# The scores' factor of 1/8 moves from the keys into the exponential for 52 of 64 heads

## The chip, the core and the metric

The kernel runs on one core of a Trainium2 chip. The core has five engines that run their own instruction streams and wait for one another through semaphores: TensorE (PE in the profile, matrix products; PEld is its loading of stationary operands), VectorE (DVE), ScalarE (ACT), GpSimd (POOL), and SyncE (SP, which here only issues DMAs). SBUF is the working memory of 128 partitions, PSUM the eight banks that TensorE writes. The metric is device time of one execution in microseconds, lower is better; a run has several executions, and their median is compared.

## The reference

The program computes causal block attention and then a mixing layer with a feed-forward network, all in fp32:

```python
scores = (1 / sqrt(64)) * q @ k.T            # 8 batches x 8 heads, 576 x 576, head size 64
scores = where(block_i >= block_j, scores, -1e9)        # blocks of 64 positions
scores = scores - max(scores, -1)
attn = exp(scores);  attn = attn / (sum(attn, -1) + 1e-9)
x = attn @ v                                 # heads side by side: 576 x 512 per batch
u = x + (x^T U V)^T                          # rank 32
out = u + relu(u @ w_ch1) @ w_ch2            # 512 -> 2048 -> 512
```

## The kernel before

**Two-part numbers.** TensorE is kept at its fast fp32r rate: an fp32 operand is split into a rounded part and a remainder (names with 1/2, h/l or hi/lo), and a product is two or three fast products. The first twelve heads (h < FS = 12) don't split q and k; their scores are one slower fp32 product out of `raw`. The 52 heads from the thirteenth on do split them.

**A head's chain.** Head h of the 64 goes through these steps, each of which is one task or a few:

- `split_qk` (L881): a DMA brings q and k, transposed, side by side into `raw` (64 partitions x 1152). For the later heads ScalarE rounds q into `q2` (L906), multiplies the half of `raw` that holds k by SCALE = 0.125 in place (L909), and rounds that into `k1` (L911). GpSimd forms the remainders `q1` (L912) and `k2` (L913), 64x576 each. Two DMAs copy `q2` and `k1` to the lower 64 partitions. The lower half of `raw` holds ones and -2^30, so that the product of one array of 128 rows adds the mask.
- `softmax` (L937): four groups of query tiles in the order (4), (3), (2), (1, 0); tile i has 128 queries (tile 0 has 64) and 128 i + 64 keys. TensorE forms the scores in a PSUM bank (L966, L967); VectorE takes the negated maximum of each row into one column of `mx`, 128 partitions x 5 (L980); ScalarE takes exp(score + `mx` column) into `p` and sums the rows into `ss` (L991).
- `normalise` (L1001): VectorE adds the 1e-9 and inverts the sums (L1007, L1008); GpSimd multiplies `p` by them (L1017).
- `transpose` (L1029, products L1050): TensorE transposes `p`; ScalarE and VectorE bring it back to SBUF as `ph` (L1027) and `pl` (L1069).
- `apply_v` (L1079, L1109): the product with v; ScalarE and VectorE join its two halves (L1115, L1117). After each second head, `mix` (L1121) does the rank-32 layer for that pair (L1134 to L1168).

**What fills TensorE.** The feed-forward network of the sixteen chunks of 288 tokens runs in two halves of the hidden layer. The first half (`ffn_chunk`, L465 and L488, banks bf and bg) is cut into tasks of six products, and these stand beside the attention as work of the lowest priority for TensorE. What of it is left when the last head is done runs alone. Then follows the second half (`block_products`, L659), whose weights are fetched and prepared (L345, L547 to L551) after the last head.

**What sets the order.** The program is written out by a planner. Every step is entered with `add(engine, ns, priority, function, reads, writes)`; `Plan.issue` (L165) then goes through time with the estimated durations `ns` and picks for each engine, whenever it is free, the ready task of the smallest priority number. The instructions are emitted in that order, so each engine's queue is fixed at build time, and engines work their queues strictly in order. A task with `port=True` or on GpSimd is never started, in the planner's account, while another such one runs. So one changed task can deal the order anew for everything behind it, on every engine.

Of the kernel before, what the change touches and what calls it, by code (L numbers as in the profile page):

```python
# [12 lines left out]
AF = mybir.ActivationFunctionType  # L13
# [4 lines left out]
S = 576  # L18
# [9 lines left out]
SCALE = 0.125  # L28
# [18 lines left out]
FS = 12  # L47
# [90 lines left out]
class Plan:  # L138
# [8 lines left out]
    def add(self, engine, ns, prio, fn, reads=(), writes=(), hold=(), after=0, port=False):  # L147

        n = len(self.tasks)
        deps = set()  # L150
        for b in reads:
            deps.update(b.writers)
            b.readers.append(n)
        for b in hold:
            deps.update(b.readers, b.writers)
        for b in writes:
            deps.update(b.readers, b.writers)
            b.writers, b.readers = [n], []
        deps.discard(n)
        slots = {b for b in (*reads, *writes) if b.pool is not None}  # L160
        for b in slots:
            b.users += 1
        self.tasks.append((engine, ns, prio, fn, deps, after, slots, port or engine == "POOL"))
# [76 lines left out]
def _act(n, sbuf=False):  # L240
    return (93 if sbuf else 52) + 0.833 * n


def _dve(n):
    return 69 + 1.042 * n
# [9 lines left out]
def attention_then_mixer(  # L255
# [10 lines left out]
    nc = tc.nc  # L266
# [8 lines left out]
    add = plan.add  # L275
# [537 lines left out]
    mx_r = [b.split(5) for b in ring(ap, 2, [P, 5], F32, "mx")]  # L813
# [23 lines left out]
    for r in vr_r:  # L837
        nc.vector.memset(r[:, 10, :], 0.0)
    for j in range(2):
        nc.vector.memset(ss_r[j][:, :, 0], 1.0)  # L840
        nc.vector.memset(ss_r[j][:, :, 1], 1e-9)
    for i, r in enumerate(pt_r):
# [38 lines left out]
    def split_qk(h, pr):  # L881
        raw, q1, k1, q2, k2 = (r[h % 2] for r in (raw_r, q1_r, k1_r, q2_r, k2_r))

        def fetch():
            if h:
                nc.sync.dma_start(out=raw[0:64, :], in_=qk[h])
            else:
                for a in (S, 0):
                    nc.sync.dma_start(out=raw[0:64, a : a + S], in_=qk[h, :, a : a + S])

        if h in (FS - 2, FS - 1):

            for n, (x, o) in enumerate(((q2, 0), (k2, S))):
                add(
                    "DVE", _dve(S) / 2, pr, lambda x=x, o=o: nc.vector.tensor_copy(x[64:P, :], raw[64:P, o : o + S]),
                    [raw], [x],
                )
        add("SP", 820, pr, fetch, writes=[raw], after=DL)
        if h < FS:
            add(  # L900
                "ACT", _act(S, True), pr,
                lambda: nc.scalar.activation(raw[0:64, S : 2 * S], raw[0:64, S : 2 * S], AF.Copy, scale=SCALE), [raw], [raw],
            )
            return
        top = slice(0, 64)
        add("ACT", _act(S, True), pr, lambda: nc.scalar.copy(q2[top], raw[top, 0:S]), [raw], [q2])  # L906
        add(
            "ACT", _act(S, True), pr,
            lambda: nc.scalar.activation(raw[top, S : 2 * S], raw[top, S : 2 * S], AF.Copy, scale=SCALE), [raw], [raw],  # L909
        )  # L910
        add("ACT", _act(S, True), pr, lambda: nc.scalar.copy(k1[top], raw[top, S : 2 * S]), [raw], [k1])  # L911
        add("POOL", 1380, pr, lambda: nc.gpsimd.tensor_sub(q1[top], raw[top, 0:S], f32(q2[top])), [raw, q2], [q1])  # L912
        add("POOL", 1380, pr, lambda: nc.gpsimd.tensor_sub(k2[top], raw[top, S : 2 * S], f32(k1[top])), [raw, k1], [k2])  # L913

        add("SP", 600, pr, lambda: nc.sync.dma_start(out=f32(q1[64:P]), in_=f32(q2[top])), [q2], [q1], after=DL)
        add("SP", 600, pr, lambda: nc.sync.dma_start(out=f32(k1[64:P]), in_=f32(k1[top])), [k1], [k1], after=DL)
# [20 lines left out]
    def softmax(h, tiles, pr):  # L937

        q1, k1, q2, k2, ss, mx = (r[h % 2] for r in (q1_r, k1_r, q2_r, k2_r, ss_r, mx_r))
        raw = raw_r[h % 2]  # L940
# [36 lines left out]
        for i, at in parts:  # L977
            add(
                "DVE", _dve(P * i + 64), pr,
                lambda i=i, at=at: nc.vector.tensor_reduce(  # L980
                    out=mx[: P if i else 64, i : i + 1], in_=view(i, at), op=ALU.max, axis=AX.XY if wide else AX.X,
                    negate=True,
                ),
                [bank], [mx.parts[i]],
            )
        for i, at in parts:
            pt, rows = pt_r[i][h % PB[i]], P if i else 64

            def exponentials(i=i, at=at, pt=pt, rows=rows):
                out = pt[:rows, : P * i + 64]  # L990
                nc.scalar.activation(  # L991
                    out.rearrange("p (j k) -> p j k", j=2) if wide else out, view(i, at), AF.Exp,
                    bias=mx[:rows, i : i + 1], accum_out=ss[:rows, i, 0:1],
                )

            add(
                "ACT", _act(P * i + 64) + 188, pr, exponentials, [bank, *(mx.parts[i] for i in tiles)],
                [pt, ss.parts[i]],
            )
# [189 lines left out]
    for h in range(NH):  # L1189
        pr = 1000.0 * h  # L1190
# [79 lines left out]
```

## Time and profile before

| | before |
|---|---|
| median of 3 runs | 1183.15 us (1181.67 to 1183.31) |
| the profiled execution | 1182.37 us, of which its span is 1180.6 us |
| granted TensorE clock, whole span | 1.00 |
| start of the mixing layer's last product (L1163), the attention's end on TensorE | 657.2 us |
| start of the second half's first product (L659) | 819.9 us |

The profile's rows give, for a group of instructions of one line, engine and tile, the number (x), the busy time, the mean duration of one in ns, and the idle time of the engine just before them with what ended it. A line that is given "out<-in" names the tiles that are written and read; sizes are partitions x elements. The windows view gives for a stretch of the span each engine's busy time in us and its number of instructions in brackets. TensorE's busy time is to be read with care: products overlap in its pipeline and their ends are modelled, so it counts as busy in small waits too; the distance from one product's start to the next one's shows more.

### The profile page before, as it was taken

How to read it: one execution, taken by the hardware profiler on the slowest of the kernel's cores; microseconds unless marked ns; L12 is line 12 of the kernel's file. 1: busy time of each engine (PE TensorE's matmuls, PEld its weight loads, DVE VectorE, ACT ScalarE, POOL GpSimd, SP SyncE). 2: the span in 40 equal slices, each digit the busy share in tenths (PEclk: the TensorE clock that was granted, in tenths of full speed). 3: DMA queues.
4: the chain of work that ended last, by engine and by line, in shares of the span. 5: the costliest groups of instructions: out<-in, count | busy, mean ns of one | idle time of the engine just before them, and what ended most of it. 6: DMA issues, size and time to landing. Idle time of an engine off the chain costs nothing.

```text
span 1180.6 us, 25204 instructions
## 1 busy us (share of the span) xinstructions
PE 1164.1 (99%) x8988; PEld 1131.4 (96%) x8988; DVE 936.2 (79%) x2009; ACT 774.9 (66%) x1924; POOL 451.2 (38%) x582
## 2 busy tenths in 40 slices
PE   9989999999999999999999999999999999999998
PEld 7778999999999999999999999999999999999998
DVE  6898887877887877777877587327989889889887
ACT  7888888989888888898887342114544444444443
POOL 5556876676757666766674122110000000000000
PEclk9999999999999999999999999999999999999999
DMA  4445565433433433443331434211132132132121
GB/s 142 141 153 154 160 177 140 116 115 108 114 112 110 123 105 111 114 117 110 112 94 52 142 113 145 66 52 50 61 122 71 51 121 70 53 121 62 60 81 41
DMA packets 75884, 122.69 MB, mean 104 GB/s; under 512 B 8944, under 2 KB 52976, under 8 KB 75760
## 3 DMA queue, kind: packets, MB, share of 16 engines
q1 hardware_dynamic: 75760, 121.09, 34.8%
q8 instruction: 71, 1.16, 0.4%
q14 instruction: 53, 0.43, 0.1%
HBM read 76.23 MB, written 29.49 MB: 90 GB/s over the span
## 4 chain that ended last, share of the span: by engine, by line
PE 81%; DVE 8%; ACT 7%; issue 2%; DMA 1%; SPq 0%; POOL 0%; ACTq 0%; DVEq 0%; POOLq 0%
PE bb L659 30%; PE bf L465 11%; PE bf L488 10%; PE ba L1050 7%; PE ba L1109 6%; PE bg L488 4%; PE bg L465 4%; ACT p L991 3%; DVE mx L980 2%; PE ba L967 2%; PE ba L966 2%; PE ba L1134 1%; PE bw L966 1%; PE ba L1148 1%; DVE pl L1069 1%
## 5 line engine op out<-in xcount | busy, mean ns | idle before, releaser
L1017 POOL TENSOR_SCALAR p<-p,rv 128x192 f32<-128x192 f32 (+4 forms) x320 | 171.8, 551 | 156.8 <-DVE rv L1008 85.2
L659 PE MATMUL bb<-hh,w1l 128*128 128x288 f32 x704 | 170.1, 295 | 0.0
L659 PE MATMUL bb<-hh,w1h 128*128 128x288 f32 x704 | 169.4, 295 | 0.0
L1069 DVE TENSOR_TENSOR pl<-ba,ph 128x512 fp32r<-128x512 f32 x216 | 113.7, 550 | 17.9 <-ACT ph L1027 15.7
L991 ACT ACTIVATE p<-ba,mx 128x448 f32<-128x448 f32 (+2 forms) x248 | 114.8, 466 | 16.4 <-DVE mx L980 12.8
L1050 PE MATMUL ba<-ident,p 128*128 128x128 f32 x768 | 122.8, 275 | 2.7 <-POOL p L1017 1.5
L659 PE MATMUL bb<-hl,w1h 128*128 128x288 f32 x576 | 123.0, 295 | 0.1
L659 PEld LDWEIGHTS bb<-hh,w1l 128*128 128x128 f32 x704 | 122.9, 190 | 0.0
L659 PEld LDWEIGHTS bb<-hh,w1h 128*128 128x128 f32 x704 | 121.9, 188 | 0.0
L488 PE MATMUL bf<-hh,w2h 128*128 128x288 f32 x384 | 118.8, 309 | 0.9 <-DVE hl L473 0.9
L488 PE MATMUL bf<-hl,w2h 128*128 128x288 f32 x384 | 113.5, 295 | 0.0
L488 PE MATMUL bf<-hh,w2l 128*128 128x288 f32 x384 | 112.7, 294 | 0.0
L447 POOL TENSOR_TENSOR ul<-ur,uh 128x288 fp32r<-128x288 f32 x72 | 61.5, 880 | 127.2 <-PE bf L465 80.9
L613 ACT CAST hh<-hb 128x576 fp32r<-128x576 f32 x98 | 65.9, 672 | 60.6 <-PE bb L659 59.3
L1027 ACT CAST ph<-ba 128x512 fp32r<-128x512 f32 x216 | 98.8, 491 | 9.1 <-PE ba L1050 7.8
L980 DVE TENSOR_REDUCE mx<-ba 128x1 f32<-128x448 f32 (+3 forms) x248 | 95.1, 406 | 10.1 <-PE ba L967 7.5
L1050 PEld LDWEIGHTS ba<-ident,p 128*128 128x128 f32 x768 | 89.9, 141 | 8.3 <-POOL p L1017 3.4
L659 PEld LDWEIGHTS bb<-hl,w1h 128*128 128x128 f32 x576 | 91.9, 188 | 0.4 <-DVE hl L614 0.4
L1109 PE MATMUL ba<-ph,vs 128*128 128x256 f32 (+3 forms) x432 | 89.9, 262 | 0.0
L465 PE MATMUL bf<-uh,w1l 128*128 128x288 f32 x392 | 82.1, 305 | 0.0
L913 POOL TENSOR_TENSOR k<-raw,k 64x576 fp32r<-64x576 f32 x52 | 75.1, 1444 | 2.1 <-POOL p L1017 0.5
L912 POOL TENSOR_TENSOR q<-raw,q 64x576 fp32r<-64x576 f32 x52 | 74.0, 1422 | 4.5 <-issue 2.1
(173 smaller groups left out, 3357.7 us busy)
## 6 DMA issues: line engine op xcount, KB each, us to landing
raw<-in_qk_dram SPq DMA_DIRECT2D x63, 288.0 KB, 3.9
st<-in_w_dram SPq DMA_DIRECT2D x32, 512.0 KB, 3.7
o_d<-ot SPq DMA_DIRECT2D x72, 144.0 KB, 1.8
vr<-in_v_dram SPq DMA_DIRECT2D x32, 320.0 KB, 3.7
ur<-u_d SPq DMA_DIRECT2D x64, 144.0 KB, 2.4
whole<-o_d SPq DMA_DIRECT2D x32, 288.0 KB, 3.1
out_dram<-whole SPq DMA_DIRECT2D x31, 288.0 KB, 2.2
ur<-u_d SPq DMA_DIRECT2D x30, 288.0 KB, 3.3
```

The costliest lines, as they stand in the source:

```text
L465: nc.tensor.matmul(ps[:, :T], w()[wn][:, k, fs], m[k].ap, start=(i == 0), stop=(i == len(ops) - 1))
L488: nc.tensor.matmul(ps[:, :T], w()[wn][:, f, ms], hs[f][x].ap, start=(i == 0), stop=(i == len(ops) - 1))
L659: nc.tensor.matmul(bank[:, i, :T], x()[:, w(k)], p.ap[:, k, :], start=first and n == 0, stop=last and n == len(ops) - 1)
L912: add("POOL", 1380, pr, lambda: nc.gpsimd.tensor_sub(q1[top], raw[top, 0:S], f32(q2[top])), [raw, q2], [q1])
L913: add("POOL", 1380, pr, lambda: nc.gpsimd.tensor_sub(k2[top], raw[top, S : 2 * S], f32(k1[top])), [raw, k1], [k2])
L980: lambda i=i, at=at: nc.vector.tensor_reduce(out=mx[: P if i else 64, i : i + 1], in_=view(i, at), op=ALU.max, axis=AX.XY if wide else AX. ...
L991: nc.scalar.activation(out.rearrange("p (j k) -> p j k", j=2) if wide else out, view(i, at), AF.Exp, bias=mx[:rows, i : i + 1], accum_out= ...
L1017: lambda x=x, rows=rows, i=i: nc.gpsimd.tensor_scalar(out=x, in0=x, scalar1=rv[:rows, i : i + 1], scalar2=1.0, op0=ALU.mult, op1=ALU.mult),
L1027: add("ACT", _act(n), pr, lambda: nc.scalar.copy(out(), inp()), reads, writes)
L1050: nc.tensor.transpose(out=bank[:, a : a + P], in_=pt_r[i][h % PB[i]][:, j * P : (j + 1) * P], identity=perm.ap)
L1069: "DVE", _dve(m), pr, lambda: nc.vector.tensor_sub(pl[:, low], bank[:, :m], f32(ph[:, low])), [bank, bh], [bl]
L1109: nc.tensor.matmul(bank[0 : c.stop, a:n], vs[:, j, c], x[:, _at(g, j)], start=(i == 0), stop=(i == len(ops) - 1))
```

## The change

For the later heads ScalarE no longer multiplies k by 1/8; the unscaled k is split. The scores then come out eight times too large, and the exponential's own factor (`scale`) brings them down: exp(0.125 score + bias). Its bias, the negated maximum, must be divided by 8 too: VectorE does that with one instruction per group of tiles, on one column of `mx` (128x1) for the groups (4), (3) and (2), on two columns (128x2) for the group (1, 0). It is entered with 150 ns and without `port`. Both `mx` buffers are cleared at the start. The first twelve heads are left as they were.

```diff
     for j in range(2):
+        nc.vector.memset(mx_r[j].ap, 0.0)
         nc.vector.memset(ss_r[j][:, :, 0], 1.0)
...
         add("ACT", _act(S, True), pr, lambda: nc.scalar.copy(q2[top], raw[top, 0:S]), [raw], [q2])
-        add(
-            "ACT", _act(S, True), pr,
-            lambda: nc.scalar.activation(raw[top, S : 2 * S], raw[top, S : 2 * S], AF.Copy, scale=SCALE), [raw], [raw],
-        )
         add("ACT", _act(S, True), pr, lambda: nc.scalar.copy(k1[top], raw[top, S : 2 * S]), [raw], [k1])
...
+        cols = slice(tiles[-1], tiles[0] + 1)
+        if h >= FS:
+
+            add(
+                "DVE", 150, pr, lambda: nc.vector.tensor_scalar_mul(mx[:, cols], mx[:, cols], SCALE),
+                [mx.parts[i] for i in tiles], [mx.parts[i] for i in tiles],
+            )
         for i, at in parts:
...
                     out.rearrange("p (j k) -> p j k", j=2) if wide else out, view(i, at), AF.Exp,
-                    bias=mx[:rows, i : i + 1], accum_out=ss[:rows, i, 0:1],
+                    bias=mx[:rows, i : i + 1], scale=SCALE if h >= FS else 1.0, accum_out=ss[:rows, i, 0:1],
                 )
```

In ScalarE's queue the thirteenth head's split stands like this now (q_0 and k_0 are q2 and k1 of an even head, L353 and L470 belong to weights and the feed-forward network; the changed kernel's line numbers are off by 1 to 4 from those of before):

```order
L907 CAST q_0_137<-raw_141 64x576
L470 ACTIVATE hh<-bf_91 128x288
L908 CAST k_0_158<-raw_141 64x576
L1119 COPY tmp_172<-ba_95 64x256
L1155 COPY tb_180<-ba_98 32x128
L353 ACTIVATE z_103<-st_101 128x512
```

Before, the same place read:

```order
L906 CAST q_0_137<-raw_141 64x576
L470 ACTIVATE hh<-bf_91 128x288
L909 ACTIVATE raw_141<-raw_141 64x576
L1115 COPY tmp_172<-ba_95 64x256
L911 CAST k_0_158<-raw_141 64x576
L1151 COPY tb_180<-ba_98 32x128
```

The multiplication of `raw` is gone, the rounding of k stands directly behind that of q and one feed-forward step, and an L353 of the weights moved ahead.

In VectorE's queue, in a head about two fifths of the way through, the last maxima of the head stood one behind the other before (mx_164 is the maxima of an even head, xl of the mixing layer):

```order
L980 TENSOR_REDUCE mx_164<-ba_97 128x1
L473 SCALAR_TENSOR_TENSOR hl<-bf_90,hh 128x288
L980 TENSOR_REDUCE mx_164<-ba_98 128x1
L980 TENSOR_REDUCE mx_164<-ba_98 64x1
L1139 TENSOR_TENSOR xl_177<-ba_96,xh_176 128x512
L1007 TENSOR_REDUCE rv_166<-ss_143 128x3
L1008 RECIPROCAL rv_166<-rv_166 128x3
```

The same head in the changed kernel (L977 is the maximum, L987 the new multiplication, L1011 and L1012 the inverse of the sums):

```order
L1073 TENSOR_TENSOR pl_170<-ba_97,ph_168 128x256
L977 TENSOR_REDUCE mx_164<-ba_95 128x1
L473 SCALAR_TENSOR_TENSOR hl<-bf_91,hh 128x288
L977 TENSOR_REDUCE mx_164<-ba_95 64x1
L987 TENSOR_SCALAR mx_164<-mx_164 128x2
L1121 TENSOR_TENSOR xt_174<-ba_98,tmp_173 64x320
L977 TENSOR_REDUCE mx_165<-bw 128x1
L1011 TENSOR_REDUCE rv_166<-ss_143 128x3
L1012 RECIPROCAL rv_166<-rv_166 128x3
```

The new instruction stands between the last maximum and everything that follows, and other work of VectorE, here L473, which waits for ScalarE, has come between the two maxima of the group.

In TensorE's queue all heads' work, the fillers and the second half have the same instructions as before, dealt anew from the first heads of the second kind on. At the last step of the attention, the mixing layer's last products, there stood before:

```order
L488 MATMUL bf_90<-hh,w2l_215 128x288
L488 MATMUL bf_90<-hl,w2h_214 128x288
L1163 MATMUL ba_96<-v_183,t_0_178 128x288
L1163 MATMUL ba_95<-v_183,t_0_178 128x288
L488 MATMUL bf_91<-hh,w2h_214 128x288
```

and now:

```order
L465 MATMUL bf_90<-ul_112,w1h_214 128x288
L465 MATMUL bf_90<-ul_113,w1h_214 128x288
L1167 MATMUL ba_97<-v_183,t_0_178 128x288
L1167 MATMUL ba_96<-v_183,t_0_178 128x288
L465 MATMUL bf_91<-uh_106,w1h_214 128x288
```

Ahead of these two there are 1848 filler products (L465 and L488) in the order before and 1932 in the order of the change: 84 more fillers stand ahead of the attention's end, and 84 fewer behind it.

## The prediction

> **What bounds the kernel now.** I read the page's first part, then the windows by stage, then TensorE's waits.
>
> ```profile
> span 1180.6 us, 25204 instructions
> PE 1164.1 (99%) x8988; PEld 1131.4 (96%) x8988; DVE 936.2 (79%) x2009; ACT 774.9 (66%) x1924; POOL 451.2 (38%) x582
> PE 81%; DVE 8%; ACT 7%; issue 2%; DMA 1%; SPq 0%; POOL 0%; ACTq 0%; DVEq 0%; POOLq 0%
> ```
>
> TensorE is busy for 99% of the span and makes up 81% of the chain that ended last. The profiled execution took 1182.37 us, 1.8 us more than its span; the median of the runs is 0.8 us higher, at 1183.15. I sum against 1182.37 and compare with 1183.15. 0.2% of that, about what a measurement of this kernel can tell from no change, is 2.4 us, so "same" runs from 1180.8 to 1185.5.
>
> The stages (stretch and its length, then busy us of PE, PEld, DVE, ACT, POOL, then clock and DMA):
>
> ```profile
> 0.00:100.00 100.00, 91.13 (x529) 74.23 (x529) 82.74 (x214) 80.91 (x225) 57.09 (x85) 1.00 0.46 142
> 100.00:640.00 540.00, 535.72 (x4408) 520.41 (x4408) 432.70 (x1150) 470.33 (x1322) 370.18 (x471) 1.00 0.42 119
> 640.00:820.00 180.00, 180.00 (x1369) 179.98 (x1368) 98.95 (x179) 56.23 (x121) 23.95 (x27) 1.00 0.29 92
> 820.00:1180.00 360.00, 357.25 (x2689) 356.77 (x2687) 321.78 (x469) 167.39 (x257) 0.00 (x0) 1.00 0.25 76
> ```
>
> The 52 later heads lie almost wholly in the second row. There ScalarE, at 87% (470.33 of 540), is the busiest of the helpers, VectorE has 80%, GpSimd 69%, and TensorE lacks only 540 - 535.72 = 4.3 us, because the feed-forward fillers stand between the heads' products. So an engine that gets faster there can give back 4.3 us by this row, perhaps twice that with the small waits that TensorE's busy time hides. Its longest waits in that stretch (sum in us, times, longest):
>
> ```profile
> PE ba L1050 <- ACT p L991: 0.9, 2, 0.6
> PE bf L488 <- DVE hl L473: 0.9, 1, 0.9
> PE ba L1050 <- DVE pl L1069: 0.7, 1, 0.7
> PE ba L1163 <- DVE ut L1168: 0.4, 2, 0.2
> PE ba L1163 <- ACT p L991: 0.3, 1, 0.3
> ```
>
> Waits that ScalarE ended are 0.9 + 0.3 = 1.2 us, those that VectorE ended 0.9 + 0.7 + 0.4 = 2.0 us.
>
> **What is removed.**
>
> ```profile
> L909 ACT ACTIVATE raw<-raw 64x576 f32<-64x576 f32 x52 | 35.7, 686 | 0.1
> ```
>
> 52 instructions of 686 ns, 35.7 us of ScalarE. Its share of the stretch falls from 87% to (470.33 - 35.7) / 540 = 80%, and a head's k is split 0.69 us earlier. No DMA comes or goes; the DMAs of q2 and k1 stay, k1's being released earlier. On the path that sets the end this is worth at most the 1.2 us that TensorE waited for ScalarE, and something of what VectorE and GpSimd pass on from it. I take **-0.6 us**, half of the 1.2, since the other half can as well come back at another place of the new order; the bounds are 0 and the stretch's 4.3 us.
>
> **What is added on VectorE.** 4 x 52 = 208 multiplications of 128x1 or 128x2 in SBUF, which the trace doesn't show. The nearest rows, with the shortest, median and longest time in ns (the inverse of the sums, also two or three columns in SBUF; the memsets of `ss`):
>
> ```profile
> L1007 DVE TENSOR_REDUCE rv<-ss x128: 128/158/160, 9.8 to 641.4; 128x2 f32<-128x4 f32 x64, 128x3 f32<-128x6 f32 x64
> L1008 DVE RECIPROCAL rv<-rv x128: 167/173/179, 10.0 to 641.6; 128x2 f32<-128x2 f32 x64, 128x3 f32<-128x3 f32 x64
> L840 DVE MEMSET ss<- x2: 62/62/62, 2.4 to 2.4; 128x5 f32 x2
> ```
>
> So between 62 and 173 ns each. I take 0.16 us, between the reduction and the reciprocal, since the reciprocal too waits for the VectorE instruction whose result it reads: 208 x 0.16 = 33 us (13 to 36). Alone this puts VectorE at (432.7 + 33) / 540 = 86%, where ScalarE is now and TensorE doesn't starve. The two new memsets (62 ns each) lie at 2.4 us, ahead of the first data, and cost nothing. The exponential itself I leave at its time: it already multiplies by a factor of 1.
>
> Then there is **the hold by GpSimd**. Some VectorE instructions last much longer while GpSimd works: line 331, which like the new one combines one SBUF tile with constants, and 1154, a small subtraction of two SBUF tiles (shortest, median and longest; then 1154's mean in the stretch, and one pair from the timeline, with start and duration):
>
> ```profile
> L331 DVE TENSOR_SCALAR z<-z x36: 175/426/2235, 7.9 to 739.9; 128x512 f32<-128x512 f32 x32, 96x288 f32<-96x288 f32 x2, 128x128 f32<-128x128 f32 x1, 128x32 f32<-128x32 f32 x1
> L1154 DVE TENSOR_TENSOR t<-tz,t x27: 280/283/1526, 111.6 to 639.3; 32x128 fp32r<-32x128 f32 x27
> L1154 DVE TENSOR_TENSOR t<-tz,t 32x128 fp32r<-32x128 f32 x27 | 10.8, 401 | 2.4 <-ACT t L1153 1.8
> 323.82 1.53 DVE L1154 TENSOR_TENSOR t<-tz,t 32x128 fp32r<-32x128 f32 x1
> 323.78 1.42 POOL L912 TENSOR_TENSOR q<-raw,q 64x576 fp32r<-64x576 f32 x1
> ```
>
> The instruction of 0.28 us took 1.53 us and ended as GpSimd's L912, begun just before it, ended. The reductions and reciprocals above never do that: their longest, 160 and 179 ns, are close to the medians. The new multiplications are of the first kind by operation, of the second by size. Bounds: none is held (0), or each meets a random moment of GpSimd, which is busy 370.18 / 540 = 69% with instructions of 370.18 / 471 = 0.79 us, so 0.69 x 0.39 = 0.27 us each, 56 us in all. I take L1154's mean excess, 401 - 283 = 118 ns, as it is the nearest small instruction that is held at all: 208 x 0.12 = 25 us. VectorE then has 432.7 + 33 + 25 = 491 us, 91%.
>
> [...]
>
> What does a hold cost at TensorE? Two long ones of VectorE, the one above and this:
>
> ```profile
> 119.52 1.57 DVE L337 SCALAR_TENSOR_TENSOR z<-st,z 128x512 int32<-128x512 int32 x1
> 119.12 1.42 POOL L912 TENSOR_TENSOR q<-raw,q 64x576 fp32r<-64x576 f32 x1
> 121.83 0.52 PE L1050 MATMUL ba<-ident,p 128*128 128x128 f32 x3 [0.70 <-DVE pl L1069]
> ```
>
> Here the `pl` behind the held instruction came late and TensorE idled 0.70 us; behind the one at 323.82 no TensorE row up to 328 us shows idle time. So a long hold costs 0.7 us at TensorE in one of two. L1154 was held that long once in 27; 208 / 27 is about 8 such holds, half of them felt: 4 x 0.7 = **+2.8 us**. Short holds are hidden by the fillers queued on TensorE. Bounds: 0, and all 8 felt in full (1.53 - 0.28 = 1.25 us): +10 us.
>
> **What is moved.** In the new VectorE order other work, some of which waits for ScalarE, comes between a group's maxima and its exponential; the exponential then starts later, and behind the waiting VectorE instruction queue the `pl`, `xt` and `rv` of other heads. What ScalarE waits for there, and VectorE in turn:
>
> ```profile
> ACT p L991 <- DVE mx L980: 19.3, 38, 2.0
> DVE rv L1007 <- ACT p L991: 20.1, 40, 1.3
> ```
>
> This is lengthened by 0.16 us in each of 208 places, 33 us, on ScalarE about what the removed L909 gives free. The orders were laid with both, and the fillers cover it: 0 in the sum, -1 to +3 as bounds (up to as much again as what VectorE makes TensorE wait, 2.0, rounded up).
>
> 84 fillers now stand ahead of the attention's end. That costs TensorE nothing, since the third window's 1369 products in 180 us make 131 ns each, wherever they stand; it moves the attention's end by 84 x 0.131 = 11 us towards the second half. What hides behind the fillers there is the preparation of the second half's weights:
>
> ```profile
> L345 DVE SCALAR_TENSOR_TENSOR whole<-st,z x16: 678/687/1182, 661.5 to 741.8; 128x512 int32<-128x512 int32 x16
> L659 PE MATMUL bb<-hh,w1h x704: 290/296/299, 819.9 to 1167.2; 128*128 128x288 f32 x176
> ```
>
> It is fetched and decoded by 742 us, and first used at 820: 78 us of cover, 67 with the 11 taken off. So this costs nothing either, up to some 400 fillers more.
>
> **The sum**: 1182.4 - 0.6 + 2.8 = 1184.6 us, 0.1% over the median before.
>
> **The rivals.**
>
> *ScalarE's relief wins.* The new instructions behave like the reciprocal and are never held, and the engine that was the busiest has 7 points less to do. For it: the rows of L1007 and L1008, and that ScalarE ends two of the five longest waits. Against: it ends only 1.2 us of them, and VectorE gets 33 us of work for the 35.7 taken. It gives half of the 4.3 us that TensorE lacks: 1180.2, and with all of it 1178.1.
>
> *VectorE becomes the bound* (the slower side). All 208 are held at a random moment of GpSimd: 432.7 + 33 + 56 = 522 us. ScalarE, the busiest now, keeps 70 us of idle in the stretch (540 - 470.33) while it waits for others; an engine that is the bound would keep less, and I take half, 35, with 0 and 70 as bounds. The stretch has room for 540 + 11 us, as the order puts 84 more fillers into it. VectorE would need 522 + 35 = 557, 6 us too many, or 41 with the full idle; the middle, 23, gives 1205.8. It decides from (551 - 35 - 433 - 33) / 208 = 0.24 us of hold each. For it: the multiplication was entered without the mark that keeps VectorE's contending instructions out of GpSimd's way in the planner's account, and L331 was held up to 1.8 us over its median. Against: L1154's mean hold is 0.12, and L1007's and L1008's is none.
>
> *The longer way to the exponential is felt.* Not VectorE's load but the later start of each exponential makes products wait, since transposes of `p` stand fixed in TensorE's queue. In the first window, where little filler stands between, TensorE lost 100 - 91.1 = 8.9 us in 100 at a load of VectorE of 83%; a loss of 4.3 us that triples gives + 8.6, 1191.0. For it: ScalarE already waits 19.3 us for maxima. Against: the order was dealt with the longer way in it, and put 84 more fillers there.
>
> *It changes nothing that is felt.* The multiplication on ScalarE was covered, so is VectorE's, and the new order loses as much as the old: 1182.4.
>
> **How the numbers follow.** Forecast (1182.4 to 1188) 0.48; relief 0.24; VectorE the bound 0.10; the longer way 0.12; nothing felt 0.06. Faster than 1180.8: 0.14 of the relief's chance. Same: 0.27 of the forecast's, 0.10 of the relief's, 0.06: 0.43. Slower than 1185.5: 0.21 of the forecast's, 0.10 and 0.12: 0.43. The forecast's own range is 1182.4 to 1188. The whole range goes from 1179.5, within the relief, to 1193, which is the forecast with all 8 holds felt in full (1192.4); outside lie most of VectorE as the bound (0.08), the relief's far end (0.05) and some of the longer way (0.05). The predicted time is the forecast's.
>
> **What would show it.** In the changed profile ScalarE should have 52 instructions and 36 us less and VectorE 208 more; the new group's mean should be 0.28 us, its shortest 0.06 to 0.17, and its long ones should end as a GpSimd instruction ends. VectorE's share of 100 to 650 us should be about 90%, TensorE should lack some 6 to 7 us there, with more waits ended by `pl` or `p`, and the windows behind 660 us should be as before. A longest near the shortest speaks for the relief, a mean over 0.4 us for VectorE as the bound. I am wrong if TensorE's idle time in the stretch falls, or if a stage outside it moves by over 2 us.

## The result, and the profile after

The change makes the kernel slower. The changed kernel took 1196.29 us (median of 4 runs, 1195.9 to 1198.88), the kernel before, run beside it, 1182.53 us (4 runs, 1181.67 to 1183.31): a ratio of 1.0117, with a 95% interval of 1.0098 to 1.0136, or 13.8 us. The forecast was 1184.6 with a range up to 1193.0, so the time lies above the range.

| | before | after |
|---|---|---|
| the profiled execution | 1182.37 us | 1196.45 us |
| attention's end on TensorE, start of the last mix product (L1163, now L1167) | 657.2 us | 682.5 us |
| first product of the second half (L659) | 819.9 us | 834.0 us |
| from there to the end of the span | 360.7 us | 360.6 us |

The first part of the page after, and its chain of work by engine:

```profile
span 1194.6 us, 25361 instructions
PE 1170.9 (98%) x8988; PEld 1132.1 (95%) x8988; DVE 987.3 (83%) x2219; ACT 750.3 (63%) x1872; POOL 449.5 (38%) x582
PE 73%; DVE 14%; ACT 8%; issue 3%; DMA 1%; SPq 0%; POOL 0%; ACTq 0%; DVEq 0%
```

TensorE's share of the chain that ended last fell from 81% to 73%, VectorE's rose from 8% to 14%. The windows view says where (stretch, length, busy us of PE, PEld, DVE, ACT, POOL, clock and DMA):

```profile
100.00:640.00 540.00, 527.76 (x4285) 507.88 (x4284) 464.71 (x1300) 428.07 (x1219) 357.40 (x454) 1.00 0.41 118
660.00:820.00 160.00, 160.00 (x1227) 159.78 (x1226) 88.37 (x172) 51.89 (x120) 24.15 (x29) 1.00 0.30 99
```

In the later heads' stretch TensorE lacks 540 - 527.76 = 12.2 us, where it lacked 4.3; busy time hides small waits, so the places where two stages begin show the loss better. The attention's end moved by 682.5 - 657.2 = 25.3 us. Of these the 84 fillers that now stand ahead of it only moved 84 x 0.131 = 11.0 us; 14.3 are lost. The second half begins 834.0 - 819.9 = 14.1 us later and lasts as long as before. So **the whole loss arises among the later heads**, and nothing behind them changed.

The new instructions by form (count, busy us, mean ns, idle time before), and then the same line in all, with shortest, median and longest:

```profile
L987 DVE TENSOR_SCALAR mx<-mx 128x2 f32<-128x2 f32 x52 | 37.3, 718 | 1.1
L987 DVE TENSOR_SCALAR mx<-mx 128x1 f32<-128x1 f32 x156 | 22.5, 146 | 1.8
L987 DVE TENSOR_SCALAR mx<-mx x208: 122/153/3582, 120.4 to 665.4; 128x1 f32<-128x1 f32 x91, 128x2 f32<-128x2 f32 x13
```

One column takes 146 ns, and the longest of the 156 took 157. Two columns take 718 ns in the mean: 149 at the shortest, 580 in the median, 39 of the 52 over 0.2 us, 17 over 0.8 us. Each of these 39 ended 18 to 32 ns after a GpSimd instruction had ended: the pair is held by GpSimd. The 52 pairs thus cost 52 x (718 - 146) = 29.7 us more on VectorE than as many single columns. What they wait for stands in the timeline (start, duration, engine and instruction; in brackets the idle time before, and its releaser):

```profile
152.46 1.42 DVE L987 TENSOR_SCALAR mx<-mx 128x2 f32<-128x2 f32 x1
153.80 0.68 DVE L337 SCALAR_TENSOR_TENSOR z<-st,z 128x512 int32<-128x512 int32 x1
154.51 0.48 DVE L1121 TENSOR_TENSOR xt<-ba,tmp 64x320 f32<-64x320 f32 x1
152.42 1.43 POOL L909 TENSOR_TENSOR q<-raw,q 64x576 fp32r<-64x576 f32 x1 [1.60 <-issue]
155.14 0.63 PE L1138 MATMUL ba<-ident,xt 128*128 128x128 f32 x4 [1.00 <-DVE xt L1121]
```

GpSimd began the next head's q remainder at 152.42 and ended it at 153.85; the pair, begun 0.04 us later, ended 0.03 us after it. Behind it stood L337 and then `xt`, for which TensorE idled 1.00 us. (Without a held pair it idles there nearly as long, see e1.) The longest hold, 3.58 us, waited through five GpSimd instructions back to back (L910, L932 and three of the four L447 that the last but one row counts):

```profile
484.49 3.58 DVE L987 TENSOR_SCALAR mx<-mx 128x2 f32<-128x2 f32 x1
483.49 1.42 POOL L910 TENSOR_TENSOR k<-raw,k 64x576 fp32r<-64x576 f32 x1
484.88 0.87 POOL L932 TENSOR_TENSOR vs<-vr,vs 128x320 fp32r<-128x320 f32 x1
485.71 3.09 POOL L447 TENSOR_TENSOR ul<-ur,uh 128x288 fp32r<-128x288 f32 x4
489.07 0.40 PE L488 MATMUL bf<-hl,w2h 128*128 128x288 f32 x1 [1.06 <-DVE hl L473]
```

The `hl` of the feed-forward network stood behind this pair, and TensorE idled 1.06 us for it.

The waits of that stretch (100 to 640 us; us in all, times, longest):

```profile
ACT p L995 <- DVE mx L987: 31.8, 53, 1.4
PE ba L1167 <- ACT p L995: 2.8, 6, 1.2
PE bf L488 <- DVE hl L473: 1.4, 2, 1.1
PE ba L1138 <- DVE xt L1121: 1.2, 2, 1.0
PE ba L959 <- DVE xt L1121: 0.9, 1, 0.9
```

The exponential waited 19.3 us for maxima before; now it waits 31.8 us for the divided ones, and TensorE's longest sum of waits is one for the exponential.

### The profile page after: what moved, and what is told of

Same layout as the page of the kernel before. It is cut to its first block, busy times and chain, and to the rows that moved or that the text cites. A ratio compares the mean times of both kernels' runs of the same rounds, so it can differ in the third digit from the quotient of the medians.

```text
span 1194.6 us, 25361 instructions
## 1 busy us (share of the span) xinstructions
PE 1170.9 (98%) x8988; PEld 1132.1 (95%) x8988; DVE 987.3 (83%) x2219; ACT 750.3 (63%) x1872; POOL 449.5 (38%) x582
## 3 DMA queue, kind: packets, MB, share of 16 engines
q1 hardware_dynamic: 75760, 121.09, 33.8%
## 4 chain that ended last, share of the span: by engine, by line
PE 73%; DVE 14%; ACT 8%; issue 3%; DMA 1%; SPq 0%; POOL 0%; ACTq 0%; DVEq 0%
PE bb L659 29%; PE bf L465 9%; PE bf L488 8%; PE ba L1054 6%; PE ba L1113 5%; PE bg L488 4%; PE bg L465 3%; DVE mx L977 3%; ACT p L995 3%; DVE pl L1073 2%; DVE mx L987 2%; PE ba L964 1%; PE ba L963 1%; PE ba L1152 1%; ACT ph L1031 1%
## 5 line engine op out<-in xcount | busy, mean ns | idle before, releaser
L659 PE MATMUL bb<-hh,w1l 128*128 128x288 f32 x704 | 170.1, 295 | 0.0
L659 PE MATMUL bb<-hh,w1h 128*128 128x288 f32 x704 | 169.4, 295 | 0.0
L995 ACT ACTIVATE p<-ba,mx 128x448 f32<-128x448 f32 (+2 forms) x248 | 115.1, 468 | 34.3 <-DVE mx L987 28.3
L659 PE MATMUL bb<-hl,w1h 128*128 128x288 f32 x576 | 123.0, 295 | 0.1
L659 PEld LDWEIGHTS bb<-hh,w1l 128*128 128x128 f32 x704 | 122.9, 190 | 0.0
L659 PEld LDWEIGHTS bb<-hh,w1h 128*128 128x128 f32 x704 | 121.9, 188 | 0.0
L488 PE MATMUL bf<-hh,w2h 128*128 128x288 f32 x384 | 119.4, 311 | 0.4 <-DVE hl L473 0.3
L488 PE MATMUL bf<-hl,w2h 128*128 128x288 f32 x384 | 113.6, 296 | 1.1 <-DVE hl L473 1.1
L488 PE MATMUL bf<-hh,w2l 128*128 128x288 f32 x384 | 112.8, 294 | 0.0
L1031 ACT CAST ph<-ba 128x512 fp32r<-128x512 f32 x216 | 101.6, 492 | 15.4 <-PE ba L1054 12.2
L447 POOL TENSOR_TENSOR ul<-ur,uh 128x288 fp32r<-128x288 f32 x72 | 60.3, 866 | 117.1 <-PE bg L465 90.6
L977 DVE TENSOR_REDUCE mx<-ba 128x1 f32<-128x448 f32 (+3 forms) x248 | 95.7, 407 | 9.6 <-PE ba L964 6.9
L659 PEld LDWEIGHTS bb<-hl,w1h 128*128 128x128 f32 x576 | 91.9, 188 | 0.4 <-DVE hl L614 0.4
L909 POOL TENSOR_TENSOR q<-raw,q 64x576 fp32r<-64x576 f32 x52 | 74.3, 1428 | 42.2 <-ACT q L907 25.5
L465 PE MATMUL bf<-uh,w1l 128*128 128x288 f32 x408 | 82.4, 301 | 0.0
L1113 PEld LDWEIGHTS ba<-ph,vs 128*128 128x128 f32 x432 | 73.2, 189 | 2.0 <-DVE ph L1080 0.4
```

Of the source, the lines that this page charges most:

```text
L465: nc.tensor.matmul(ps[:, :T], w()[wn][:, k, fs], m[k].ap, start=(i == 0), stop=(i == len(ops) - 1))
L488: nc.tensor.matmul(ps[:, :T], w()[wn][:, f, ms], hs[f][x].ap, start=(i == 0), stop=(i == len(ops) - 1))
L659: nc.tensor.matmul(bank[:, i, :T], x()[:, w(k)], p.ap[:, k, :], start=first and n == 0, stop=last and n == len(ops) - 1)
L977: lambda i=i, at=at: nc.vector.tensor_reduce(out=mx[: P if i else 64, i : i + 1], in_=view(i, at), op=ALU.max, axis=AX.XY if wide else AX. ...
L995: nc.scalar.activation(out.rearrange("p (j k) -> p j k", j=2) if wide else out, view(i, at), AF.Exp, bias=mx[:rows, i : i + 1], scale=SCAL ...
L1031: add("ACT", _act(n), pr, lambda: nc.scalar.copy(out(), inp()), reads, writes)
```

## The experiments

Two theories stood against each other. **The hold**: what costs is the pair of two columns, held by GpSimd. **The link**: what costs is that one more dependent step stands between a maximum and its exponential, whatever its form; beside it the bare load of 208 instructions, or the order dealt anew, could cost. The diffs are against the changed kernel; each ratio is against the kernel before on the same chip, which lay between 1182.04 and 1183.03 us. It is estimated from all executions, and can differ by a thousandth from the ratio of the two medians. "Fillers" are the feed-forward products ahead of the last mix product, "end" is the start of that product.

### The new order's own cost, and the pair (e3, e2, e1, e6)

e3 emits nothing for the division, in the same order:

```diff
-            add(
-                "DVE", 150, pr, lambda: nc.vector.tensor_scalar_mul(mx[:, cols], mx[:, cols], SCALE),
-                [mx.parts[i] for i in tiles], [mx.parts[i] for i in tiles],
-            )
+            add("DVE", 150, pr, lambda: None, [mx.parts[i] for i in tiles], [mx.parts[i] for i in tiles])
```

> The changed kernel's order without any of the 208 divisions, which leaves the maxima of the later heads undivided. What remains is ScalarE's relief and the new order. Theory H: 1181 to 1185 us, and little below the run without the pairs alone. Theory L: it falls clearly below the run without the pairs alone, by some 8 us. Theory O: 1190 us or more although VectorE has nothing added.

1183.49 us, 1.0012 (1.0002 to 1.0021), end at 669.7 us. The order, with ScalarE's relief in it, is not what costs 13.8 us, but it brings no gain either.

e2 divides single columns only:

```diff
+            def divide():
+                if len(tiles) == 1:
+                    nc.vector.tensor_scalar_mul(mx[:, cols], mx[:, cols], SCALE)
...
```

> The changed kernel without the 52 divisions of the pair (1, 0): the 156 of 128x1 stay, and the maxima of tiles 1 and 0 are left undivided. Theory H: 1183 to 1187 us, as with two single ones or a little less. Theory L: a quarter of the divisions less, so about a quarter of the 13.8 us back, 1192 to 1194 us. Theory O: no gain, 1194 us or more.

1187.54 us, 1.0046 (1.0031 to 1.0061), end at 672.2 us. The 156 single columns, none of them held, cost some 4 us over e3. The hold theory had expected little between these two runs: there is more than the hold.

e1 divides the pair as two single columns:

```diff
+            def divide():
+                for i in tiles:
+                    nc.vector.tensor_scalar_mul(mx[:, i : i + 1], mx[:, i : i + 1], SCALE)
...
```

> The changed kernel, where the pair of columns of the group (1, 0) is divided by two instructions of 128x1 in place of one of 128x2; the order of every other instruction is that of the change. Theory H (the 128x2 form alone is held by GpSimd's instructions, 37.3 us for 52 against 22.5 us for 156 of the 128x1 form, and these holds are what TensorE feels): no instruction of line 987 lasts over 0.2 us, VectorE's time for the divisions falls from 60 to about 38 us, and the time to 1183 to 1187 us. Theory L (the load on VectorE and the longer way to the exponential cost the time, held or not): 1193 us or more, since 52 instructions more are issued in the same places. Theory O (the order dealt anew is the worse one, whatever the divisions last): 1193 us or more.

1187.97 us, 1.0053 (1.0038 to 1.0068), end at 674.3 us. The same values, the same order of the other instructions, 52 instructions more, and 8 us less than the changed kernel; that is one microsecond above the hold theory's range. The group of e1, and its timeline at the place shown above:

```profile
L988 DVE TENSOR_SCALAR mx<-mx 128x1 f32<-128x1 f32 x260 | 33.8, 144 | 1.9
```

```profile
154.76 0.26 DVE L988 TENSOR_SCALAR mx<-mx 128x1 f32<-128x1 f32 x3
154.94 1.85 DVE L337 SCALAR_TENSOR_TENSOR z<-st,z 128x512 int32<-128x512 int32 x1
154.82 1.42 POOL L909 TENSOR_TENSOR q<-raw,q 64x576 fp32r<-64x576 f32 x1 [1.69 <-issue]
```

GpSimd's L909 begins at 154.82, in the midst of three divisions that take 0.26 us together; they run through, and the exponential can start. It is the large L337 behind them, a preparation of weights, that is held now, 1.85 us instead of 0.68. Over the whole run L337 means 820 ns in e1 and 711 after the change, 36 x 0.109 = 3.9 us: a part of the 29.7 us has only moved between the two. At this place that gains nothing, for `xt` stands behind L337 in both, and TensorE idles 0.91 us for it in e1.

The gain lies elsewhere. TensorE's products stand in the same order in both runs, so they can be laid side by side: at 150 us the changed kernel is 2.3 us ahead of e1, at 675 us it is 8.2 us behind. The lag grows in many steps. The largest are 1.2 us at 489.07, where TensorE waits for the `hl` behind the hold of 3.58 us, 1.0 us at 584.01, where a product of the mixing layer waits for an exponential, and 0.7 us at 387.55, where a transpose waits for VectorE's `xl` of the mixing layer.

e6 issues each pair a second time, on a spare tile:

```diff
+                if len(tiles) == 2:
+                    nc.vector.tensor_scalar_mul(spare[:, 0:2], spare[:, 2:4], SCALE)
```

> The changed kernel with a second multiplication of 128x2 right behind each of the 52 pairs, on a spare tile that nobody reads; all else in the same order. Theory H: the second one finds GpSimd at its next instruction and is held too, by 0.3 to 0.6 us on average; 1203 to 1212 us. Theory L: 52 more instructions of 0.15 us at most, 8 us of VectorE spread over the stretch; 1197 to 1199 us. Theory O: 1196 to 1198 us.

1204.61 us, 1.0185 (1.0168 to 1.0202), 8.3 us over the changed kernel. The granted clock of its four executions was 0.996 to 0.999 instead of 1.00, so some of that may be the clock's. The groups:

```profile
L989 DVE TENSOR_SCALAR mx<-mx 128x2 f32<-128x2 f32 x52 | 37.3, 717 | 1.1
L991 DVE TENSOR_SCALAR spare<-spare 128x2 f32<-128x2 f32 x52 | 14.0, 268 | 0.0
```

A pair directly behind a held one mostly goes through: of the spare ones only 5 took over 0.2 us. So 14.0 us more on VectorE, over half of it plain work, made 8.3 us: the doubling hit the number without the repeated hold that was to make it, and it doesn't measure the price of a hold.

### The load against the link (e11, e12)

e11 issues the 156 single instructions on a spare tile, so that the exponential waits for the maximum alone. e12 divides the single columns in place and issues the pair on the spare tile (the comments at the right name the run):

```diff
+                if len(tiles) == 1:                                                     # e11
+                    nc.vector.tensor_scalar_mul(spare[:, 0:1], spare[:, 2:3], SCALE)    # e11
...
+                else:                                                                   # e12
+                    nc.vector.tensor_scalar_mul(spare[:, 0:2], spare[:, 2:4], SCALE)    # e12
```

> The changed kernel and its order, without the pairs, and with the 156 single instructions put on a spare tile, so that no exponential waits for them; the later heads' maxima stay undivided. With the divisions in these places it took 1187.5, without any 1183.5. Load (the 4 us of the single divisions come from VectorE's time): 1186.5 to 1188 us. Link (they come from the longer way from a maximum to its exponential): 1183 to 1184.5 us.

1183.46 us, 1.0012 (1.0002 to 1.0023): as e3, with 156 instructions more. Its group, its wait, and the wait in e2, where the same 156 stand in the chain:

```profile
L990 DVE TENSOR_SCALAR spare<-spare 128x1 f32<-128x1 f32 x156 | 22.5, 144 | 1.4
```

```profile
ACT p L998 <- DVE mx L979: 10.1, 15, 1.8
```

```profile
ACT p L996 <- DVE mx L988: 22.1, 36, 1.5
```

22.5 us of load on VectorE cost nothing. The same instructions in the chain make the exponential wait 22.1 us, and 2.4 more for undivided maxima, instead of 10.1 us, and cost 1.0046 - 1.0012, 4 us. That is the link.

Two things are to be kept in mind. The sum of the exponential's waits is no price: it was 19.3 us in the kernel before, and is 24.9 us in e10 below, which loses next to nothing. The largest step of e2's lag behind e11 is 0.8 us at 371.11, where a product of the mixing layer waits 0.66 us for an exponential; the others are small. And a dependent division also stops VectorE for a moment: 47 of the 156 stand directly behind a maximum, and these start 34 ns after its end in e2 and 82 ns before it in e11 (medians), some 5 us of VectorE in all. As 22.5 us of load cost nothing, this is hardly where the 4 us come from, but no run shows the two apart.

> The changed kernel and its order, with each of the 52 pair instructions of 128x2 put on a spare tile that nobody reads, so that the exponentials of tiles 1 and 0 don't wait for it; their maxima stay undivided, the 156 single divisions stay. Without the pairs it took 1187.5, with them 1196.3. Theory H, through the queue (a held instruction stops everything behind it in VectorE's queue, whoever reads its result): 1194 to 1197 us, with a mean of the 128x2 form over 0.5 us. Theory H, through the link (only the exponentials that wait for the pair are late): 1187 to 1190 us.

1190.94 us, 1.0076 (1.0059 to 1.0093), between both numbers. The spare pairs are held like the real ones:

```profile
L992 DVE TENSOR_SCALAR spare<-spare 128x2 f32<-128x2 f32 x52 | 33.6, 646 | 0.1
```

Over e2 it is 0.0030, 3.5 us (the intervals still touch): what the held pair does to the work queued behind it on VectorE. The remaining 0.0041 up to the changed kernel, 4.8 us, comes with the exponential of the last group waiting for the held pair. How the two divide is uncertain: the granted clock was 0.997 or 0.998 in three of e12's four executions, and the one at 1.00 took 1189.04 us, 1.5 us over the middle of e2's two at 1.00 (1187.28 and 1187.79). That leaves 1.5 to 3.5 us for the queue, and the larger part for the exponential.

### The order of before (e8, e4, e5) and an order without room (e10)

In these the planner deals as before, since ScalarE's step stays in its account and issues nothing; e8 has no division at all, e4 puts 260 single ones directly behind their maxima without room in the account, e5 has the pair in place of the two last singles (the comments name the run):

```diff
+        add("ACT", _act(S, True), pr, lambda: None, [raw], [raw])
...
+                if h >= FS:                                  # e4
+                    nc.vector.tensor_scalar_mul(mx[:, i : i + 1], mx[:, i : i + 1], SCALE)    # e4
...
+                if h >= FS and i == tiles[-1]:               # e5
+                    nc.vector.tensor_scalar_mul(mx[:, cols], mx[:, cols], SCALE)              # e5
```

> The kernel before in its own order, with the 52 multiplications of k on ScalarE left out, the factor in the exponential, and no division of the maxima, which stay undivided for the later heads. It shows ScalarE's relief alone; the new order without divisions took 1183.5 beside 1182.0 before. Theory R (the relief is worth something, and the new order takes it back): 1180 us or less. Theory N (TensorE did not wait for ScalarE, the relief is worth nothing, and the new order costs 1.5 us by itself): 1181.5 to 1182.5 us.

1184.7 us beside 1183.03, 1.0008 (0.9998 to 1.0019), above both ranges: in this order taking 35.7 us off ScalarE is worth nothing.

> The changed kernel without any division, and with an order that the planner deals without room for them; the later heads' maxima stay undivided. It shows what a way to divide that costs nothing could reach at best. If ScalarE's relief can be had in an order of its own: 1178 to 1181 us. If the relief is worth nothing in any order: 1182 to 1185 us, as in the two orders tried.

1183.16 us, 1.0014 (1.0002 to 1.0027), with 1824 fillers ahead of the end at 653.5 us; here the task of the division is gone and the order is dealt without it. With e3 and e8 these are three runs without any division, in three orders, 0.8 to 1.4 thousandths above the kernel before: no order here turns ScalarE's relief into time. In e10 the excess goes with the clock: its five executions at a granted clock of 1.00 have a median of 1181.80 us, where the kernel before on that chip has 1182.00, and its three at 0.997 or 0.998 took 1186.4 to 1187.0. In e3 it stays: 1183.46 against 1181.86 us at 1.00.

> The kernel before in its own order, with the change's arithmetic: the multiplication on ScalarE left out, and behind each maximum of a later head its division, one instruction of 128x1 each, 260 in all, for which the order has laid no room. Theory H (holds of the pairs are the most, single divisions cost a few us by the longer way): 1185 to 1190 us. Theory O (the new order is what costs): at most 1184 us.

1204.48 us, 1.0175 (1.0157 to 1.0192), end at 678.5 us, far above both ranges. Without room the single divisions cost more than the whole change does. The timeline of e4 shows what one of them takes:

```profile
300.07 0.22 DVE L1075 TENSOR_TENSOR ph<-ba,ph 64x64 fp32r<-64x64 f32 x1
300.32 0.49 DVE L977 TENSOR_REDUCE mx<-ba 128x1 f32<-128x320 f32 x1
300.85 0.15 DVE L982 TENSOR_SCALAR mx<-mx 128x1 f32<-128x1 f32 x1
300.92 0.45 DVE L473 SCALAR_TENSOR_TENSOR hl<-bf,hh 128x288 fp32r<-128x288 f32 x1
```

The division starts only 0.04 us after the maximum ended, and ends 0.19 us after it. Over the run a division that stands directly behind its maximum ends 188 ns after it, and what follows starts 71 ns after the division's start, where an instruction that needs no such result starts 76 ns before the maximum's end. So each costs VectorE 34 + 71 + 76 = 181 ns, and 260 of them 47 us. Whether TensorE loses its 20 us through this load or through the later exponentials isn't shown here; e13 below says more.

> The same, but tiles 1 and 0 are divided together by one instruction of 128x2 behind the later of the two maxima, as the change does it; 208 divisions. Theory H: the pairs are held by GpSimd in this order too, by 0.27 us or more on average, and the time is 4 to 10 us above the run with single divisions in this order. Theory O: the same as that run or less, since there are 52 instructions fewer.

1212.47 us, 1.0238 (1.0222 to 1.0255), 8 us over e4. The groups of e5:

```profile
L983 DVE TENSOR_SCALAR mx<-mx 128x1 f32<-128x1 f32 x156 | 24.0, 154 | 5.3
L983 DVE TENSOR_SCALAR mx<-mx 128x2 f32<-128x2 f32 x52 | 18.8, 361 | 1.8
```

Here 24 of 52 pairs took over 0.2 us, the longest 1.82. Their 18.8 us stand against 104 x 0.154 = 16.0 us of the singles that they replace, and yet the run takes 8 us more: not the sum on VectorE counts but the long ones, each of which is the last link before an exponential. A part can have another cause, which no run here takes out: e4 divides tile 1 directly behind its own maximum, e5 only behind that of tile 0, so the exponential of tile 1 waits for both.

### Three attempts at a better form (e7, e9, e13)

e7 enters the pair with the planner's mark for instructions that contend with GpSimd (`port=len(tiles) == 2`):

> The changed kernel with the pair's division marked as one that contends with GpSimd, so that the planner never starts it beside a GpSimd task; the order is dealt anew by that. Theory H: the mean of the 128x2 form falls from 718 ns to under 450, and the time to 1185 to 1191 us. Theory L (load and longer way): no change beyond 2 us, 1194 to 1198 us.

1197.62 us, 1.0111 (1.0094 to 1.0128): no help, though its four executions had a granted clock of 0.994 to 0.997. The pair still means 635 ns, 26 of them over 0.2 us:

```profile
L987 DVE TENSOR_SCALAR mx<-mx 128x2 f32<-128x2 f32 x52 | 33.0, 635 | 0.7
```

The mark keeps the two apart in the planner's own time only. Why the real times drift so far from it isn't shown.

e9 lets one instruction form maximum and division: a multiplication by -1/8 that accumulates its minimum, the products going to a spare tile.

```diff
+            nc.vector.tensor_scalar(
+                out=o.rearrange("p (j k) -> p j k", j=2) if wide else o, in0=view(i, at), scalar1=-SCALE,
+                scalar2=1e30, op0=ALU.mult, op1=ALU.min, accum_out=mx[:rows, i : i + 1],
...
```

> A version meant to do better: VectorE takes the maximum and its division in one instruction for the later heads, a product of the scores with -1/8 whose minimum goes to mx, while the products themselves go to a spare tile; no division of its own, no multiplication on ScalarE, and the order that the planner deals without either. If the instruction lasts as long as the maximum did (406 and 749 ns on average) and is not held: 1182 to 1186 us. If it adds an instruction of its own for reading the result, some 0.1 to 0.2 us in 260 places: 1188 us or more, as single divisions in an order without room for them.

1188.91 us, 1.006 (1.0045 to 1.0075). The profile shows a second instruction behind each:

```profile
L983 DVE TENSOR_SCALAR_CACHE_REDUCE junk<-ba 128x448 f32<-128x448 f32 x52 | 32.2, 620 | 3.7 <-PE ba L965 1.6
L983 DVE DVE_READ_ACCUMULATOR junk<-ba 128x1 f32 x156 | 12.8, 82 | 0.0
```

The instruction itself lasts as long as the maximum did (617 ns for this form in e10). Reading the accumulator takes 82 ns behind each of the 128-row maxima, so the additional step of the chain is still there. TensorE, ScalarE and GpSimd work in e10's order here, and the difference to e10, 0.0046 or 5.4 us, is what this step costs.

e13 joins each single division with its maximum into one task and lays 200 ns of room for it:

```diff
+                if h >= FS:
+                    nc.vector.tensor_scalar_mul(mx[:, i : i + 1], mx[:, i : i + 1], SCALE)
...
+            add("DVE", _dve(P * i + 64) + (200 if h >= FS else 0), pr, maxima, [bank], [mx.parts[i]])
```

> The change's arithmetic with single divisions, each in one task with its maximum, so that the planner can put nothing between the two, and lays 200 ns of room for each (in the old order a division directly behind its maximum ended 188 ns after it); 260 divisions, the order dealt anew. Gap theory (the 4 us of the 156 single divisions come from other VectorE work that the planner puts between maximum and division): 1183 to 1186 us. Length theory (any division lengthens the way to the exponential and is paid for, about 20 ns a piece, wherever it stands): 1187 to 1190 us. Load theory (47 us of VectorE's time, 0.18 us a piece, in place of the 34 of two singles): 1190 us or more.

1186.2 us, 1.0026 (1.0015 to 1.0037), the best form of the change, and still slower than the kernel before. On VectorE it is dearer than e1:

```profile
L981 DVE TENSOR_SCALAR mx<-mx 128x1 f32<-128x1 f32 x260 | 40.0, 154 | 8.9
```

40.0 us instead of 33.8, and yet half of e1's loss is gone. The gap to e1 is 0.0027, and the intervals lie just apart. In e1 the planner set other work between a maximum and its division: from the end of the maximum last ahead of it in VectorE's queue to its own end a division takes 466 ns in the mean there, and 188 ns in e13. That this is the reason is argued, since the order is dealt anew too. Set beside e4, e13 points to what room is worth: the same 260 divisions, each ending 188 ns behind its maximum, cost 1.0175 where the order was laid without them and 1.0026 where it was laid with 200 ns for each.

### The account

| from | to | ratio | us |
|---|---|---|---|
| before | order dealt anew, ScalarE relieved (e3) | 1.0012 | 1.4 |
| e3 | 156 single divisions in the chain (e2) | 1.0046 | 4.0 |
| e2 | two more singles in place of the pair (e1) | 1.0053 | 0.8 |
| e1 | the pair as 128x2, held by GpSimd (after) | 1.0117 | 7.6 |

The us are the differences of the ratios times 1182.5. The intervals of e3 and e2 lie apart, and so do those of e1 and the changed kernel; the first step is just above nothing, and the third is within the error. The last step is the clearest: the same values by one instruction instead of two, with the order of all others unchanged.

## Why the prediction was wrong, point by point

**What bounds the kernel** was read rightly: TensorE, among the later heads, through waits for its helpers. The windows behind 660 us are as forecast, and VectorE has 464.7 / 540 = 86% of its stretch (about 90% was forecast). TensorE lacks 12.2 us there, about twice the 6 to 7 forecast.

**The relief of ScalarE** (-0.6, with up to -4.3 as bound) is nothing in e8 and e10. The time that the removed instruction gave free became idle time of ScalarE. The rival in which the relief wins fell with it.

**The length of the multiplication** was sized well, 0.16 us against 0.146. The total of the holds, 25 us forecast and 29.7 measured, came out by luck: it was spread over all 208, and lies on 52. So the mean of all 208, forecast at 0.28 us, is (37.3 + 22.5) / 208 = 0.29, while the distribution behind it is another. The bare load costs nothing, as the sum had it (e11).

**The hold's cost at TensorE is one of the two steps that failed, by its size.** The prediction took from L1154, held that long once in 27, that 8 of the 208 would be held long, and let TensorE feel half of them by 0.7 us: 2.8 us. The holds lie on the 52 pairs alone, 17 of them over 0.8 us, 0.57 us in the mean, and the time grows by 7.6 us for 29.7 us of holds. Each stands as the last link before an exponential, where L1154, from which the price came, does not. Of the two ways by which it is felt, the forecast counted only the one, work queued behind it (1.5 to 3.5 us by e12 over e2); the exponential that waits for the pair itself (4.8 us or more up to the changed kernel) wasn't in the term. The upper bound of 10 us was taken from 8 holds of 1.25 us, and contains the 7.6.

Which of the 208 are held shows by their form: the pairs mean 718 ns, the single columns 146, and none of these was held, though 96 of the 156 began while a GpSimd instruction ran. The prediction's bound for a single hold, 0.27 us by a random moment of GpSimd, was half of the 0.57 measured on the pairs, for two reasons. A random moment falls more often into a long instruction than into a short one; the durations of GpSimd's 471 instructions in that stretch of the kernel before give 0.35 us. And the moment isn't random: in 22 of 52 the q remainder of the next head (L909, 74 us in all) was running when the pair began, where chance would give about 7.

**The longer way to the exponential is the other step that failed.** It was put at 0, within -1 to +3. It costs 4 us for 156 single columns (e2 against e11), and 4.8 for 260. "The fillers cover it" was the wrong part: the runs show that a later exponential does cost time where the same instructions beside the chain don't. The rival built on this gave 1191.0, + 8.6; its mechanism is at work with half of its price.

**The order dealt anew** was put at 0 and lies at 1.4 us with the relief in it. That e10, in an order without room for the divisions, has no excess at a clock of 1.00, and e3 has 1.6 us, points to the change's order. It isn't shown to be the cause: e8, in the order of before, lies 0.8 thousandths up too, and its six executions at 1.00 fall apart into 1182.3 to 1182.5 and 1184.9 to 1185.1 us, for which no run here gives a reason.

**The 84 fillers** moved the attention's end by their 11 us and cost nothing, as forecast; the other 14.3 us of that shift are the loss. (The 67 us of cover are room for 511 fillers at 131 ns, not for some 400; nothing hung on it.)

**VectorE as the bound** (1205.8, all 208 held) didn't happen: none of the 156 single columns was held, the longest took 157 ns. e4 shows how near that side was: without room in the order 260 single columns cost 1.75%.

Put together, two terms of the sum came out as 7.6 and 4.0 + 0.8 where it had 2.8 and 0, and 1.4 us of loss stood where it had 0.6 of gain: 1184.6 + 4.8 + 4.8 + 2.0 = 1196.2 us. Either of the two terms alone would have left the time within the range.

## What to carry to other kernels

An instruction is to be priced by who waits for its result, not by its share of its engine: 22.5 us on VectorE cost nothing beside the chain and 4 us in it. Before small fp32 columns are put together into one VectorE instruction beside a busy GpSimd, the two forms are to be tried: here two instructions of one column were 7.6 us better than one of two. A step that is added to a planned order is to be entered with the time that it really takes: the same 260 divisions cost 3 us with room and 20 without. And work taken from the busiest of the helpers brought nothing here, because TensorE hardly waited for it (1.2 us).

## What the runs showed of the hardware

- For this multiplication one column more decides on the hold: the 128x1 form in SBUF took 122 to 157 ns, though 96 of the 156 began while a GpSimd instruction ran, and in the same stretch the 128x2 form took 149 to 3582 ns. It isn't so for every instruction of two columns: the reciprocal of 128x2 took 167 to 171 ns in the same run, and 20 of the 64 began while a GpSimd instruction ran.
- A held instruction doesn't always come next when GpSimd's instruction ends: the pair that began at 484.49, while L910 ran, let L932 and three of the four L447 pass as well, 3.58 us in all.
- The pair directly behind a held pair mostly isn't held: 268 ns in the mean against 717, and 5 of 52 over 0.2 us against 39 (e6).
- The factor in the exponential is all but free: L995 of 128x448 and its narrower forms mean 468 ns with the factor in 52 of 64 heads, 466 before.
- A division directly behind its maximum, whose result it reads, started 34 ns after the maximum's end, where an instruction that needs no such result started 76 ns before it (e4, medians).
